# Short filler matmuls, weight and beacon loads asked for in another order, and query copies of batch 1 on ScalarE, in a fused beacon attention and maxout FFN kernel

## The chip, the cores and the metric

The kernel runs on one core of a Trainium2 chip. The metric is device time in microseconds, the median of several runs. The engines are called as the profile calls them: PE (TensorE, matmuls; PEld is its weight loads), ACT (ScalarE), DVE (VectorE), POOL (GpSimd) and SP (SyncE, here an issuer of DMAs). Each works through its own instructions in order, and they meet at semaphores.

## The reference

Attention over 8 batches of 8 heads, 576 tokens of 64 features, with 16 beacon keys and values in front of each head's own, causal over the own ones; then an FFN over 4608 tokens whose hidden layer is the largest of three products.

```python
def _attn_ref(q, k, v, beacon_k, beacon_v):      # B, H, S, Nb, D = 8, 8, 576, 16, 64
    scale = 1.0 / np.sqrt(D)
    k_all = np.concatenate([beacon_k, k], axis=2)
    v_all = np.concatenate([beacon_v, v], axis=2)
    scores = scale * np.matmul(q, k_all.transpose(0, 1, 3, 2))
    causal[:, Nb:] = np.triu(np.ones((S, S), dtype=bool), k=1)
    scores = np.where(causal, -1000000000.0, scores)
    scores = scores - scores.max(-1, keepdims=True)
    a = np.exp(scores)
    a /= a.sum(-1, keepdims=True) + 1e-09
    return np.matmul(a, v_all)

def _moe_ref(x, w1, w2, w3, w_out):              # 4608 tokens, 512 -> 768 -> 512
    h = np.maximum(np.maximum(x @ w1, x @ w2), x @ w3)
    return h @ w_out
```

All inputs and the output are float32; the kernel's matmuls are in bfloat16.

## The kernel before

**Tiling.** Two heads are a pair (four pairs a batch, numbered through: pairs 0 to 3 are batch 0, 4 to 7 batch 1), four heads a quad. For a pair, queries and keys come from HBM with tokens on the partitions and are turned by PE transposes into qT and kT (features on the partitions); the turned tile is in a PSUM bank and is copied to SBUF by DVE or ACT. Scores come out with keys on the partitions (L505 in batch 0, L520 later), ACT takes the exponential of a whole group of banks into `at_sb` (L514, L538), and masks zero what is above the diagonal: POOL with an affine select (L560), or DVE with a product by a triangle (L558, batch 0 only). For a quad, PE forms the sums of the weights, with a block of ones as stationary operand, and the products with the values (L609 in batch 0, L642 later). ACT gets the reciprocal of the sums by Ln and Exp (L675 and L676, or L658 to L660), and DVE multiplies it in and leaves the attention output in `xT` (L686, L665), which is already the layout that the FFN wants. The FFN works on blocks of 512 tokens in units: mm1 units (L710, in halves L739 for the first block) with a running maximum in `hT` by DVE (L728, L751; the first of the three products is only cast, L730, L753), and mm2 units (L762) whose result is copied to `y` and stored.

**Order.** Nothing is scheduled by a program: the order in which the Python code emits instructions is the order on each engine, and it is written out by hand. `start()` loads and turns the first two pairs of batch 0. `first_batch()` is a list of calls: `S_` scores and exponential of a pair's group, `T` (`turn_part`) a half turn of a pair, `M` masks (a third argument True puts them on DVE), `P` (`emit_pv`) sums and value products of a quad's half, `V(t)` (`cast_first_v`) the cast of value tile t by POOL, `F` an FFN unit. `second_batch()` goes over pairs 4 to 7: beacon keys of the next pair copied by ACT, a burst of scores with five exponentials, masks on POOL, the turn of the next pair, two or three FFN units; then sums and products of quad 2 (`emit_pv_whole`) and the turn of pair 8. From pair 8 on a loop does the same with a plan of loads and casts, and there the query copy of a turned pair is by ACT already.

**Queues around the change.** POOL casts the values, masks, and also issues the DMAs that cast on their way from float32 to bfloat16: `load_w(i, [g])` (half g of FFN weight i, L344), `load_cast(p)` (queries and keys of pair p, L258). SP issues the value loads (L301, L306) and the beacon keys of batches 1 to 3 (L353), which POOL casts at L968. What POOL waits for holds up all that stands behind it in its list, asks for DMAs included.

**Fillers.** `fill(at_bank, n)` (L413) runs n matmuls of a tile of ones into a PSUM bank that is about to be overwritten; `turn_part` calls it with `idle` 1 in four places (L920, L923, L928, L935), and `first_batch` with 2 in two (L941, L950).

**Turned queries.** `turn_pair(p, q_copy)` (L458) takes two banks, emits 24 transposes, has DVE copy the keys (`evac_k`, L453) and `q_copy` the queries (`evac_q`, L442). `second_batch` gives it `by_dve`. `emit_pv_whole` (L623) emits the matmuls of a quad, then three ACT copies of the products to `raw` (L652, L653), then Ln, Ln and Exp on ACT (L658 to L660), and returns `finish`, which emits the two multiplies on DVE.

Of the kernel before, what the change touches and what calls it, by code (L numbers as in the profile page):

```python
# [17 lines left out]
def kernel(  # L18
# [41 lines left out]
    n_quad = 2  # L60
    PPB = H // 2
# [41 lines left out]
    def head(g, j):  # L103
        return 4 * g + j

    def place(p):
        b, pi = divmod(p, PPB)
        return b, pi // PPQ, 2 * (pi % PPQ)
# [15 lines left out]
    acc = psum.tile([128, N_BANK, 512], FP32, name="acc")  # L124
# [20 lines left out]
    def next_bank():  # L145
        i = free_banks.pop(0)
        free_banks.append(i)
        return i
# [18 lines left out]
    def next_psum(dtype=FP32):  # L167
        view = acc[:, next_bank()]
        return view if dtype == FP32 else view.bitcast(dtype)
# [9 lines left out]
    bk32_1 = const.tile([NB_PE - Nb, H, D], FP32, name="bk32_1")  # L179
    bk16_1 = const.tile([NB_PE - Nb, H, D], BF16, name="bk16_1")  # L180
# [3 lines left out]
    busy = const.tile([128, 512], BF16, name="busy")  # L184
# [20 lines left out]
    by_dve = nc.vector.tensor_copy  # L205
    by_act = nc.scalar.copy
    by_pool = nc.gpsimd.tensor_copy
# [46 lines left out]
    def load_cast(p):  # L254
        b, g, j0 = place(p)
        for i, src in enumerate((q, k)):
            t16 = quads[g][i][:, 2 * j0 : 2 * j0 + 4]
            nc.gpsimd.dma_start(  # L258
                out=t16.rearrange("p (h s) r d -> p h (s r d)", h=2),
                in_=src[b, head(g, j0) : head(g, j0) + 2].rearrange("h (p r) d -> p h (r d)", r=QR),  # L260
            )
            rows = t16.rearrange("p (h s) r d -> p h (s r) d", h=2)
            stage["pair16", p, i] = (rows[:, 0], rows[:, 1])
# [77 lines left out]
    def load_w(i, gs=range(n_quad)):  # L341
        wv = (moe_w1, moe_w2, moe_w3)[i].rearrange("(g p e) f -> g p e f", g=n_quad, e=2)
        for g in gs:
            nc.gpsimd.dma_start(out=w_in[i][:, 2 * g : 2 * g + 2], in_=wv[g])  # L344
# [66 lines left out]
                )  # L411

    def fill(at_bank, n):  # L413
        for _ in range(n):
            nc.tensor.matmul(
                acc[:, at_bank], busy[:, 0:128], busy, start=True, stop=True
            )

    def turn_part(p, h, i, at_bank, copy=None, idle=0):
# [31 lines left out]
    def evac_k(p, ps, copy):  # L451
        kT = kTs[p % NT]
        copy(  # L453
            kT[:, Nb:NK].rearrange("d (p r) -> d p r", r=QR),
            ps.rearrange("d (r p) -> d p r", r=QR),
        )

    def turn_pair(p, q_copy):  # L458
        banks = [next_psum(BF16)[:, 0:S] for i in range(2)]
        for i in range(2):  # L460
            turn(p, i, banks[i])
        evac_k(p, banks[1], by_dve)
        evac_q(p, banks[0], q_copy)
# [156 lines left out]

    products = []

    def emit_pv_whole(quad):  # L623
        b, g = divmod(quad, n_quad)
        v_sb = v_tiles[b]
        for p in range(PPQ * quad, PPQ * (quad + 1)):
            assert all((p, gi) in masked for gi in range(NG))
        banks = [next_bank() for _ in range(4)]
        runs = [(part, banks[part], 0, HEAD, S) for part in range(3)]
        runs += [(part, banks[3], part * HEAD, 0, HEAD) for part in range(3)]  # L630
        for part, bank, lo, qa, qb in runs:
            ts = [t for t in range(n_kt) if q_min[t] < qb]
            for t in ts:
                q0 = max(qa, q_min[t])
                n = k_rows[t]
                for j in range(4):
                    lhsT = (
                        ones[0:n]
                        if part == 0
                        else v_sb[0:n, t, head(g, j), part - 1 : D : 2]  # L640
                    )
                    nc.tensor.matmul(  # L642
                        acc[32 * j : 32 * j + 32, bank, lo + q0 - qa : lo + qb - qa],
                        lhsT,
                        at_view(PPQ * quad + j // 2, t, j % 2, q0, qb),
                        start=(t == 0),
                        stop=(t == ts[-1]),
                        tile_position=(0, 32 * j),
                    )
        raw = pv_pool.tile([128, 2, S], FP32, name="raw")  # L650
        for part in (1, 2):
            nc.scalar.copy(raw[:, part - 1, HEAD:S], acc[:, banks[part]])  # L652
        nc.scalar.copy(  # L653
            raw[:, :, 0:HEAD],
            acc[:, banks[3], HEAD : 3 * HEAD].rearrange("p (i c) -> p i c", i=2),
        )
        recip = nrm_pool.tile([128, S], FP32, name="recip")
        nc.scalar.activation(out=recip[:, HEAD:S], in_=acc[:, banks[0]], func=AF.Ln)  # L658
        nc.scalar.activation(out=recip[:, 0:HEAD], in_=acc[:, banks[3], 0:HEAD], func=AF.Ln)
        nc.scalar.activation(out=recip, in_=recip, func=AF.Exp, scale=-1.0)  # L660

        def finish():
            c0 = b % RING * S
            for i in range(2):
                nc.vector.tensor_mul(xT[:, 2 * g + i, c0 : c0 + S], raw[:, i], recip)  # L665
            if g == n_quad - 1:
                ready[0] = 2 * b + 1

        return finish
# [168 lines left out]
    def L(fn, *a):  # L838
        return lambda: fn(*a)
# [68 lines left out]
    def first_batch():  # L908
        S_(0, 0)
        T(2, 0, 0, 6)  # L910
        T(3, 0, 0, 4)
        load_v(0, 0, nc.vector)
        load_v(0, 1)
        load_beacons(1, B_PE, bk32_1)
        S_(1, 0)
        T(2, 0, 1, 7)
        T(3, 0, 1, 5)
        M(0, 0, True)
        S_(2, 0)
        T(0, 1, 0, 6, None, 1)  # L920
        T(1, 1, 0, 4)
        S_(3, 0)
        T(0, 1, 1, 7, None, 1)  # L923
        T(1, 1, 1, 5)
        M(1, 0, True)
        S_(0, 1)
        V(0)
        T(2, 1, 0, 6, None, 1)  # L928
        T(3, 1, 0, 4)
        load_w(0, [0])  # L930
        S_(1, 1)
        M(2, 0, True)
        V(1)
        load_w(0, [1])
        T(2, 1, 1, 7, None, 1)  # L935
        T(3, 1, 1, 5)
        M(3, 0, True)
        S_(0, 3)
        V(2)
        S_(0, 2)  # L940
        fill(6, 2)  # L941
        S_(1, 3)
        for p in range(PPB):
            M(p, 1)
        M(0, 3, True)
        M(0, 2, True)
        V(3)
        V(4)
        S_(1, 2)
        fill(6, 2)  # L950
        S_(2, 1)
        M(1, 3, True)
        M(1, 2, True)
        S_(3, 1)
        load_w(1, [0])
        P(0, 0, apart=True)
        S_(2, 3)
        load_w(1, [1])
        M(2, 3)
        S_(2, 2)  # L960
        M(2, 2)
        P(0, 1, 0, 2)
        S_(3, 3)
        M(3, 3, True)
        P(0, 1, 2)
        S_(3, 2)
        M(3, 2, True)
        by_pool(bk16_1, bk32_1)  # L968
        load_cast(PPB)
        load_cast(PPB + 1)  # L970
        load_cast(PPB + 2)
        load_w(2)
        load_cast(PPB + 3)
        P(1, 0, tiles=sc_psum.tile())
        P(1, 1, tiles=sc_psum.tile())
        for quad, hf in ((0, 0), (1, 0), (0, 1), (1, 1)):
            invert_sums(quad, hf)
            multiply()
            if (quad, hf) == (0, 1):
                F()  # L980
        F(2)
        turn_beacons(1, B_PE, bk16_1)
        place_beacons(PPB, by_act)
        F(2)
        free_banks[:] = [4, 5, 0, 1, 2, 3, 7, 6]
        turn_pair(PPB, by_act)
        load_v(1, 0, nc.vector)
        load_v(1, 1)
        F(1, next_psum)

    def second_batch():
        for p in range(PPB, 2 * PPB):
            place_beacons(p + 1, by_act)
            emit_burst(p)
            if p == PPB + 2:
                load_cast(2 * PPB)
                load_w_out()
                load_cast(2 * PPB + 1)
            for gi in range(NG):
                emit_masks(p, gi)  # L1000
                if p == PPB + 2 and gi == 1:
                    cast_v(1, 0, by_pool)
            if p == PPB + 2:
                next_load(gate=nc.gpsimd)
                next_load(4)
                cast_v(1, 1, by_pool)
            if p + 1 < 2 * PPB:
                turn_pair(p + 1, by_dve)
                F(2, next_psum)
                if p < PPB + 2:  # L1010
                    F(1, last_pair(), True)
        F(2, next_psum)
        finish = emit_pv_whole(n_quad)
        turn_pair(2 * PPB, by_dve)
        F(2, next_psum)
        finish()

# [92 lines left out]
```

## Time and profile before

| | us |
|---|---|
| runs, median of 3 | 284.77 (284.46 to 284.79) |
| profiled execution, device time | 286.59 |
| profiled execution, span of the instructions | 284.9 |

The span is the time from the first to the last instruction of the program; the device time of the same execution has 1.7 us around it. The TensorE clock that was granted is 1.00 in every stage. The stages of the profiled execution, as busy microseconds of each engine:

| stage, us from the start | PE | DVE | ACT | POOL |
|---|---|---|---|---|
| 7 to 16: first scores and turns of batch 0 | 7.75 | 8.67 | 8.45 | 2.15 |
| 16 to 22: sums and products of batch 0 | 4.66 | 1.23 | 4.58 | 3.97 |
| 22 to 26: up to the first FFN unit | 2.04 | 3.08 | 2.36 | 2.32 |
| 26 to 45: FFN units, pairs 4 to 6 | 18.57 | 13.25 | 11.38 | 11.58 |
| 45 to 60: pair 7, quads 2 and 3 | 14.75 | 8.32 | 12.68 | 10.93 |
| 60 to 270: the rest of the loop | 210.00 | 128.32 | 117.58 | 98.04 |

How lines of the profile are read: in a timeline, the first number is the start in us and the second how long the group took; then engine, line, operation, the tile written and the tile read by the program's names, the partitions and elements, and how many instructions the group merges (the shape is that of the first). In brackets stands how long the engine had been idle before, and what released it, as far as semaphore events show; where that had long been done, it was something else. In the DMA part, a queue's line gives packets, megabytes and its share of the time of 16 DMA engines. POOL's and SP's DMA lines give the time to issue; the landing comes later.

### The profile page before, as it was taken

What the parts mean: (1) busy time and instruction counts of PE and PEld (TensorE: products, weight loads), DVE (VectorE), ACT (ScalarE), POOL (GpSimd) and SP (SyncE); (2) the same over time, 40 slices, a digit from 0 to 9 for tenths busy, and PEclk for the clock granted to TensorE, in tenths of its full rate; (3) what the DMA queues carried; (4) which work ended last, traced back from release to release, by engine and by line L of the source; (5) the groups of instructions that cost most, each with busy time, mean ns of one, the idle gap of its engine ahead of it and who ended that gap; (6) DMA issues with size and microseconds to landing.
All of it is one profiled execution on the core that took longest, in us unless ns stands there. A gap on an engine that the chain in (4) does not pass through costs nothing.

```text
span 284.9 us, 7772 instructions
## 1 busy us (share of the span) xinstructions
PE 274.5 (96%) x3075; PEld 157.3 (55%) x3075; DVE 173.7 (61%) x311; ACT 159.9 (56%) x299; POOL 134.2 (47%) x277
## 2 busy tenths in 40 slices
PE   7976999999999999999999999999999999999994
PEld 3545774555555555555556787555555554444442
DVE  4936785564765748373837383638364847776872
ACT  3975568895668585858585858575766640000000
POOL 7167359558486775457455836583336210000000
PEclk9999999999999999999999999999999999999999
DMA  8999999999998999979999999979845003003004
GB/s 139 204 165 166 170 211 144 239 175 294 286 209 213 226 257 193 183 185 275 252 223 193 257 210 203 205 183 267 206 104 171 0 2 147 4 0 147 2 0 147
DMA packets 85316, 48.84 MB, mean 171 GB/s; under 512 B 64416, under 2 KB 80032, under 8 KB 85280
## 3 DMA queue, kind: packets, MB, share of 16 engines
q1 hardware_dynamic: 78176, 42.22, 65.5%
q0 software_dynamic: 6544, 5.80, 13.9%
q8 instruction: 24, 0.39, 0.6%
q10 hardware_dynamic: 560, 0.33, 0.5%
q14 instruction: 12, 0.10, 0.2%
HBM read 35.13 MB, written 14.22 MB: 173 GB/s over the span
## 4 chain that ended last, share of the span: by engine, by line
PE 81%; DVE 1%; issue 0%; DVEq 0%
PE acc L710 45%; PE acc L762 16%; PE acc L642 11%; PE acc L520 7%; PE acc L406 2%; PE acc L780 0%; DVE hT L728 0%; DVE y L787 0%; DVE qT L442 0%; DVE kT L453 0%; DVEq L453 0%
## 5 line engine op out<-in xcount | busy, mean ns | idle before, releaser
L710 PE MATMUL acc<-xT,w_sb 128*128 128x512 bf16 (+4 forms) x744 | 135.5, 338 | 0.1
L728 DVE TENSOR_TENSOR hT<-hT,acc 128x512 bf16<-128x512 bf16 x102 | 70.0, 688 | 58.2 <-PE acc L710 53.2
L710 PEld LDWEIGHTS <-w_sb 128*128 128x128 bf16 x744 | 69.2, 98 | 59.6
L560 POOL TENSOR_SCALAR_AFFINE_SELECT at_sb<-at_sb 128x256 bf16<-128x256 bf16 (+1 forms) x171 | 61.9, 384 | 81.0 <-ACT at_sb L538 79.8
L538 ACT ACTIVATE at_sb<-acc 128x208 bf16<-128x208 f32 (+3 forms) x140 | 89.5, 737 | 6.7 <-PE acc L520 5.5
L762 PE MATMUL acc<-w_out_sb,hT 128*128 128x512 bf16 (+2 forms) x246 | 48.4, 348 | 0.0
L277 POOL CAST p<-st 96x768 bf16<-96x768 f32 x44 | 34.9, 822 | 0.0
L769 DVE COPY y<-acc 128x512 f32<-128x512 f32 (+1 forms) x35 | 22.0, 629 | 21.2 <-PE acc L762 14.9
L762 PEld LDWEIGHTS <-hT 128*128 128x128 bf16 x246 | 22.6, 98 | 21.7 <-DVE hT L728 1.6
L730 ACT CAST hT<-acc 128x352 bf16<-128x352 f32 x18 | 8.1, 452 | 47.0 <-PE acc L710 47.0
L730 DVE CAST hT<-acc 128x512 bf16<-128x512 f32 (+1 forms) x48 | 26.6, 554 | 9.9 <-PE acc L710 9.6
L520 PE MATMUL acc<-qT,kT 64*128 64x208 bf16 (+1 forms) x336 | 26.6, 280 | 0.4 <-DVE hT L728 0.2
L787 ACT COPY y<-acc 128x320 f32<-128x320 f32 x1 | 0.4, 425 | 46.0 <-PE acc L780 46.0
L642 PE MATMUL acc<-at_sb,v_sb 128*32 128x512 bf16 (+5 forms) x672 | 22.8, 281 | 0.0
L520 PEld LDWEIGHTS <-kT 64*128 64x128 bf16 x336 | 15.4, 94 | 12.7 <-issue 2.5
L665 DVE TENSOR_TENSOR xT<-raw,recip 128x576 bf16<-128x576 f32 x28 | 21.1, 796 | 0.0
L642 PEld LDWEIGHTS <-v_sb 128*32 128x32 bf16 (+1 forms) x672 | 14.6, 97 | 6.7
L322 POOL CAST v_sb<-st 128x1536 bf16<-128x1536 f32 (+2 forms) x21 | 18.3, 894 | 0.0
L652 ACT COPY raw<-acc 128x512 f32<-128x512 f32 x28 | 15.8, 637 | 2.6 <-PE acc L642 2.4
L642 PE MATMUL acc<-at_sb,ones 128*32 128x512 bf16 (+3 forms) x336 | 14.9, 284 | 0.0
L514 ACT ACTIVATE at_sb<-acc 128x1024 bf16<-128x1024 f32 (+2 forms) x16 | 13.1, 864 | 2.6 <-PE acc L505 2.5
L453 DVE COPY kT<-acc 128x576 bf16<-128x576 bf16 x12 | 9.0, 754 | 5.7 <-PE acc L406 4.5
(73 smaller groups left out, 179.4 us busy)
## 6 DMA issues: line engine op xcount, KB each, us to landing
out_dram<-y SPq DMA_DIRECT2D x35, 256.0 KB, 3.5
st<-in_q_dram SPq DMA_DIRECT2D x22, 288.0 KB, 4.4
st<-in_k_dram SPq DMA_DIRECT2D x22, 288.0 KB, 4.7
st<-in_v_dram SPq DMA_DIRECT2D x24, 256.0 KB, 6.0
w_sb<-in_moe_w_dram POOLq DMA_DIRECT2D x6, 384.0 KB, 7.8
q_dram<-p SPq DMA_DIRECT2D x16, 144.0 KB, 2.6
k_dram<-p SPq DMA_DIRECT2D x16, 144.0 KB, 2.5
st<-in_v_dram SPq DMA_DIRECT2D x8, 224.0 KB, 6.2
```

The source lines that it names most:

```text
L277: cast(t16.rearrange("p r h d -> p h r d"), st[0:QP, i * NQ2 : (i + 1) * NQ2].rearrange("p (h r d) -> p h r d", h=2, r=QR),)
L322: cast(v_sb[0:n, t:t1].rearrange("p t h d -> p (t h d)"), st[0:n, (t - t_lo) * H * D : (t1 - t_lo) * H * D],)
L520: nc.tensor.matmul(ps, kTs[p % NT][hs, 128 * t : 128 * t + 128], qTs[p % NT][hs, q0:q1], start=True, stop=True, tile_position=(64 * e, 0),)
L538: nc.scalar.activation(out=both_heads(p, gi)[:, e0:e1], in_=acc[:, first + e0 : first + e1, 0 : g_width(p, gi)], func=AF.Exp, scale=scale,)
L560: nc.gpsimd.affine_select(out=view, in_=view, compare_op=ALU.is_ge, fill=0.0, base=x0, pattern=[[0, 2], [1, hi - lo]], channel_multiplier=-1,)
L642: nc.tensor.matmul(acc[32 * j : 32 * j + 32, bank, lo + q0 - qa : lo + qb - qa], lhsT, at_view(PPQ * quad + j // 2, t, j % 2, q0, qb), sta ...
L665: nc.vector.tensor_mul(xT[:, 2 * g + i, c0 : c0 + S], raw[:, i], recip)
L710: nc.tensor.matmul(ps[:, a:b], w_in[i][:, ct, 128 * ft : 128 * (ft + 1)], xT[:, ct, x0 : x0 + b - a], start=(ct == 0), stop=(ct == n_ct - 1),)
L728: nc.vector.tensor_max(h[:, lo:hi], h[:, lo:hi], ps[:, lo:hi])
L730: (by_act if hi < TOKB else by_dve)(h[:, lo:hi], ps[:, lo:hi])
L762: nc.tensor.matmul(ps[:, lo:hi], hT[:, ft, 128 * tt : 128 * (tt + 1)], w_out_sb[:, ft, lo:hi], start=(ft == 0), stop=(ft == n_ft - 1),)
L769: (by_act if hi < d_model else by_dve)(y[:, lo:hi], ps[:, lo:hi])
```

## The change

It has four parts. (1) A filler of 512 columns becomes four of 128, each into its own quarter of the bank; all have a weight load of their own. (2) In `first_batch` the first half of weight 1 (`load_w(0, [0])`) is asked for behind `V(1)` and no longer ahead of the second scores of pair 1; so it moves behind that cast on POOL. (3) The halves of weight 2 (`load_w(1, ...)`) move by a few calls to either side of the masks `M(2, 3)` and `M(2, 2)`, and the beacon cast moves behind the casting loads of pairs 4 and 5. (4) In `second_batch` the turned queries of pairs 5 to 8 are copied by ACT; the turn of pair 8 is now emitted from inside `emit_pv_whole`, so that on ACT its copy stands between the copies to `raw` and the logarithms.

```diff
     def fill(at_bank, n):
-        for _ in range(n):
+        for i in range(4 * n):
+            x0 = 128 * (i % 4)
             nc.tensor.matmul(
-                acc[:, at_bank], busy[:, 0:128], busy, start=True, stop=True
+                acc[:, at_bank, x0 : x0 + 128],
+                busy[:, 0:128],
+                busy[:, 0:128],
+                start=True,
+                stop=True,
             )
...
-    def emit_pv_whole(quad):
+    def emit_pv_whole(quad, after_raw=None):
...
             acc[:, banks[3], HEAD : 3 * HEAD].rearrange("p (i c) -> p i c", i=2),
         )
+        if after_raw:
+            after_raw()
         recip = nrm_pool.tile([128, S], FP32, name="recip")
...
         T(3, 1, 0, 4)
-        load_w(0, [0])
         S_(1, 1)
         M(2, 0, True)
         V(1)
+        load_w(0, [0])
         load_w(0, [1])
...
         S_(3, 1)
-        load_w(1, [0])
         P(0, 0, apart=True)
         S_(2, 3)
-        load_w(1, [1])
+        load_w(1, [0])
         M(2, 3)
         S_(2, 2)
         M(2, 2)
+        load_w(1, [1])
         P(0, 1, 0, 2)
...
-        by_pool(bk16_1, bk32_1)
         load_cast(PPB)
         load_cast(PPB + 1)
+        by_pool(bk16_1, bk32_1)
         load_cast(PPB + 2)
...
             if p + 1 < 2 * PPB:
-                turn_pair(p + 1, by_dve)
+                turn_pair(p + 1, by_act)
                 F(2, next_psum)
                 if p < PPB + 2:
                     F(1, last_pair(), True)
         F(2, next_psum)
-        finish = emit_pv_whole(n_quad)
-        turn_pair(2 * PPB, by_dve)
+        finish = emit_pv_whole(n_quad, L(turn_pair, 2 * PPB, by_act))
         F(2, next_psum)
         finish()
```

## The prediction

> **What bounds it now.** I read first the page's busy shares, its slices and its DMA queues, then the timelines of PE, ACT, POOL and DVE up to 60 us, then the DMA view in narrow windows.
>
> ```profile
> span 284.9 us, 7772 instructions
> PE 274.5 (96%) x3075; PEld 157.3 (55%) x3075; DVE 173.7 (61%) x311; ACT 159.9 (56%) x299; POOL 134.2 (47%) x277
> PE   7976999999999999999999999999999999999994
> q8 instruction: 24, 0.39, 0.6%
> ```
>
> From the fourth slice on PE is the bound: whatever brings PE to its first FFN matmul (L739, 26.27 us) earlier comes off the end, unless a later wait eats it. Up to 26 us PE waits for others, and there most of the edits lie. The POOL timeline of that stretch:
>
> ```profile
> 13.77 0.56 POOL L344 DMA_DIRECT2D w_sb<-in_moe_w_dram  x1
> 15.00 0.61 POOL L334 CAST v_sb<-st 128x512 bf16<-128x512 f32 x1 [0.68 <-DMA st<-in_v_dram]
> 15.55 0.55 POOL L344 DMA_DIRECT2D w_sb<-in_moe_w_dram  x1
> 16.09 1.36 POOL L334 CAST v_sb<-st 128x512 bf16<-128x512 f32 x2
> 19.48 0.61 POOL L334 CAST v_sb<-st 80x512 bf16<-80x512 f32 x1 [2.03 <-DMA st<-in_v_dram]
> 20.03 1.06 POOL L344 DMA_DIRECT2D w_sb<-in_moe_w_dram  x2
> 23.74 0.60 POOL L968 CAST bk<-bk 48x512 bf16<-48x512 f32 x1 [1.68 <-DMA bk<-in_beacon_k_dram]
> ```
>
> The fifth value cast waits 2.03 us for its DMA. PE, ACT and DVE in the same stretch:
>
> ```profile
> 20.14 0.22 PE L609 MATMUL acc<-at_sb,v_sb 80*32 80x80 bf16 x4 [0.49 <-POOL v_sb L334]
> 20.72 1.30 ACT L514 ACTIVATE at_sb<-acc 128x992 bf16<-128x992 f32 x2 [1.24 <-PE acc L505]
> 21.75 0.76 DVE L558 TENSOR_TENSOR at_sb<-at_sb,tri 128x160 bf16<-128x160 bf16 x3 [4.77 <-ACT at_sb L514]
> 22.44 0.63 PE L609 MATMUL acc<-at_sb,ones 128*32 128x288 bf16 x14
> 25.03 0.27 PE L609 MATMUL acc<-at_sb,ones 128*32 128x208 bf16 x4 [1.96 <-DVE xT L686]
> 26.27 2.86 PE L739 MATMUL acc<-xT,w_sb 128*128 128x256 bf16 x24
> ```
>
> The largest wait, 1.96 us, is in the middle of the row sums of P(1, 1). DVE is named, but these matmuls read no xT, and the masks that they do read were done at 21.75 + 0.76 = 22.51. So I look for something else, and find it in queue q8. Its 24 packets of 0.39 MB are 16 KB each; PE has 3075 matmuls and 3075 weight loads, and 6150 / 24 = 256 to a packet. Counted along the timeline, the wait sits behind matmul 352 and its load, some 706 instructions in, and the narrow DMA windows show q8 packets at 11.92, 22.78 (until 23.73), 26.80 and 35.62 us. I read the wait as PE's **instruction block** coming late: it ends 1.30 us after the second packet does. Blocks of 256 then end at 194, 450 and 706, if 62 instructions run ahead of the program's first (706 + 62 = 3 x 256), which no row shows. PE came past 450 at 18.77, at the earliest 18.3 by its waits, and the packet started 4.5 us later; for the next five it is 4.5, 5.0, 1.4, 4.2 and 4.5.
>
> In batch 1:
>
> ```profile
> 42.30 3.20 ACT L538 ACTIVATE at_sb<-acc 128x208 bf16<-128x208 f32 x5 [1.26 <-PE acc L520]
> 44.45 0.75 DVE L442 COPY qT<-acc 128x576 bf16<-128x576 bf16 x1
> 45.34 0.24 ACT L449 COPY kT<-bT 128x16 bf16<-128x16 bf16 x1
> 45.58 1.23 PE L520 MATMUL acc<-qT,kT 64*128 64x208 bf16 x12
> 54.30 0.36 PE L520 MATMUL acc<-qT,kT 64*128 64x336 bf16 x5 [0.20 <-DVE hT L728]
> ```
>
> The query copy of pair 7 is done at 45.20, before its scores at 45.58; ACT is busy with exponentials until 45.50.
>
> **The change, part by part.**
>
> *Fillers.* Eight of 512 columns (L415 x8) become 32 of 128. Two in a row take 0.60 us where one takes 0.387: 213 ns each, start to start. For 128 columns with a weight load each there is no row. L406 with 96 columns gives (680 - 206) / 11 = 43 ns, L739 with 256 gives (2860 - 273) / 23 = 112 ns. Between them I take 57: four are 228, so 15 ns more a filler, 0.12 us in all; bounds 8 x (172 - 213) = -0.33 and 8 x (448 - 213) = +1.9 us. PE waits for exponentials right behind them, 0.21, 0.39 and 0.53 us at 14.45, 15.92 and 18.34, and ACT is busy 8.45 of 9.00 us from 7 to 16: on the path 0 at 57 ns, and 1.9 - 1.1 = 0.8 at the upper bound. But they add 24 matmuls and 24 loads, 48 PE instructions, ahead of everything from 15 us on.
>
> *Weight 1 behind V(1).* POOL would now do V(1) at 15.00, both asks at 15.55 and 16.10, V(2) and V(3) from 16.65 to 18.0. These two casts are 0.56 later, and P(0, 0) wants the third value tile at about 16.85: PE stops there until 17.33. The cover is ACT, whose exponentials run on to 19.48; the scores behind it come at 17.9, before their exponential is due at 18.2: 0, or 0.5 without that cover. On the DMA side, value packets fall from 601 in the microsecond at 14 to 156 and 16 in the next two, as soon as the first weight packets come (49 and 60 of 3 KB). Some 730 value and 384 beacon packets are then left; at 800 a microsecond, the rate at 10 to 14, they are through at 16.5, ahead of the weight's first packets at 15.55 + 1.2. So V(4) follows V(3), 18.0 to 18.6 in place of 19.48 to 20.09. The 0.49 wait at 20.14 goes, and exponentials, sums and P(1, 0) come 0.5 earlier. Weight 1 lands at 16.8 + 0.79 MB / 0.19 to 0.20 MB per us = 20.7 to 21.0 (23.25 before), well before L739.
>
> *Weight 2, casting loads, beacon cast.* POOL: half of weight 2 at 18.6, masks at 19.2, the other half at 20.1, four casting loads of 0.64 each from 20.65, the beacon cast at 23.2 (23.74 before), which PE wants at 29.07. Nothing is later. The transposes at 31.33 show no wait for their loads, so nothing is won either.
>
> *The instruction block.* With 48 more instructions the block ends fall on what were 402 and 658. 402 lies in P(0, 0) behind the third value tile: PE passes it at 17.33, 1.0 earlier than 18.3. 658 lies at the end of P(1, 0), reached at some 22.2 - 0.5 = 21.7. The packet asked for at 17.33 stands behind all of weight 1, which drains at 20.7 to 21.0; I take 21.0 (bounds: 1.4 behind the request, 18.7, and 5.0 behind it, 22.3). PE goes on 0.95 + 1.30 later, at 23.25. From there it has 0.25 of P(1, 0) and 1.85 of P(1, 1) to do: L739 at 25.35, 0.92 before 26.27. The reciprocal of (1, 0), which now starts after the stop, needs 0.25 + 0.1 + 0.41 + 0.44 + about 1 of multiplies = 2.2 and is wanted 2.4 after it by the last of the first unit's four matmuls: it just fits.
>
> *Copies by ACT.* Pairs 5 and 6: exponentials end at 36.4 and 40.9, the copy (0.62 to 0.69) and the beacon copy at 37.2 and 41.8, the scores start at 37.46 and 41.94: no cost. Pair 7 has two FFN units between, not three: the copy runs 45.36 to 46.0, scores at 46.06 in place of 45.58, +0.48; the bank wait inside them (0.14) goes, and DVE, 0.75 freer, takes 0.08 out of the scores of pair 5. Pair 8: ACT does the copy at 51.6 before the logarithms, which end at 53.56, just before the exponentials at 53.65; DVE's two hT steps start 0.5 earlier, so the wait at 54.30 goes, -0.29 (from 54.30 back to the matmul before it are 0.50 us, and 0.21 where such a pair doesn't wait). Net 0.48 - 0.14 - 0.08 - 0.29 = -0.03, between -0.5 and +0.5.
>
> **Sum:** -0.92 - 0.03 = -0.95 us: span 284.9 to 283.95, the profiled execution's 286.59 to 285.64. The median of the runs, 284.77, is 1.8 below that; I take the same difference off it: **283.8**.
>
> [...]
>
> **Rivals.**
>
> 1. *The stop follows what the profile names.* For it: the first xT multiply of (0, 1) starts at 24.67, and may end just before 25.03. Against it: that product is not read there. The stop would then come with the reciprocals, 0.5 earlier through V(4): 284.77 - 0.5 = 284.3.
> 2. *Slower: the block is as late as before, and stops more.* Weight 1's halves now stand in the queues as one run, right before the request. If the packet starts at 22.78 again, PE goes on at 25.03 from 658, not 706, with 2.1 to do in place of 1.24: +0.86, 285.6. It decides from a packet at 21.9 on. For it: 4.5 to 5.0 in most of the loaded cases. Against: values and beacons, which shared the engines from 17 to 23, are through by then.
> 3. *No stop:* the packet starts by 19.4. L739 follows P(1, 1) at 23.07 + 1.25 - 0.5 = 23.8, -2.4: 282.4. For it the 1.4 case; against it a queue full of weights.
>
> **Chances.** Forecast 0.43, first rival 0.2, second 0.2, third 0.17. 0.2% is 0.57 us, about what a measurement of this kernel can tell from no change. Faster by more: the third, most of the forecast, a little of the first: 0.58. Within: 0.23. Slower: 0.19, the second. The forecast's own range is 283.2 to 284.5 (packet at 20.4 to 21.7); the range is 282.4 to 285.5, which takes in rivals 1 and 3 and the 0.8 of the fillers' bound, and leaves out the worst of the second.
>
> **What would show it.** Right: the fifth value cast at about 18 us with no DMA wait; the q8 packet at about 21; a PE stop inside P(1, 0), not in P(1, 1), ending near 23.3; L739 near 25.3; the scores of pair 7 waiting some 0.5 for an ACT copy; no wait in those of pair 8. Wrong: the stop still at the same matmul, a cast of V(4) that still waits, or a later stop of PE that gives the gain back.

## The result, and the profile after

The kernel became slower: 287.43 us, the median of 15 runs (285.55 to 289.63), against 285.13 of 15 runs of the kernel before (284.46 to 286.28). The ratio of the means is 1.0065, with a 95% interval of 1.0037 to 1.0092. The forecast was 283.8, and the time lies above its range.

And yet the profiled execution of the changed kernel looks much as forecast: span 284.3 us against 284.9, device time 286.00 against 286.59. Its page:

```profile
span 284.3 us, 7821 instructions
PE 274.2 (96%) x3099; PEld 158.1 (56%) x3099; DVE 171.7 (60%) x307; ACT 162.1 (57%) x303; POOL 134.5 (47%) x277
PE   7987999999999999999999999999999999999994
q8 instruction: 24, 0.39, 0.6%
```

PE has its 24 matmuls and 24 loads more, ACT four copies more, DVE four fewer; the share of PE and the slices have hardly moved. POOL's timeline:

```profile
15.43 1.11 POOL L344 DMA_DIRECT2D w_sb<-in_moe_w_dram  x2
16.52 1.89 POOL L334 CAST v_sb<-st 128x512 bf16<-128x512 f32 x3
18.35 0.53 POOL L344 DMA_DIRECT2D w_sb<-in_moe_w_dram  x1
23.25 0.62 POOL L977 CAST bk<-bk 48x512 bf16<-48x512 f32 x1
```

The last three value casts are one run of 1.89 us with no DMA wait in it; before, the fifth stood 2.03 us. PE's timeline:

```profile
21.36 0.53 PE L614 MATMUL acc<-at_sb,v_sb 128*32 128x288 bf16 x18
23.44 0.33 PE L614 MATMUL acc<-at_sb,v_sb 128*32 128x176 bf16 x8 [1.56 <-issue]
25.23 2.86 PE L746 MATMUL acc<-xT,w_sb 128*128 128x256 bf16 x24
30.37 0.39 PE L746 MATMUL acc<-xT,w_sb 128*128 128x256 bf16 x2 [0.23 <-issue]
45.44 0.89 PE L525 MATMUL acc<-qT,kT 64*128 64x208 bf16 x12 [0.42 <-ACT qT L447]
52.80 1.21 PE L525 MATMUL acc<-qT,kT 64*128 64x208 bf16 x12
```

The stop has moved from P(1, 1) into P(1, 0) and is 1.56 us, with nothing to be seen that PE waits for ("issue"); the q8 packets start at 11.55, 21.08, 28.02 and 34.05 us. The first FFN matmul is at 25.23 (26.27 before). A second, small stop has come at 30.37. The scores of pair 7 wait 0.42 for ACT's copy, and the wait at 54.30 is gone.

So the two profiled executions say 0.6 us faster and the medians 2.3 slower. What lies between is in the list of all runs. The difference of device time and span is about 1.75 us in all of them. The kernel before has spans around 283.4 us, and its profiled execution (span 284.9, device time 286.59) lies above all 15 of its runs. The changed kernel has 7 runs around 284.3 at a granted clock of 1.00, and 8 at 285.7 to 287.9 whose mean clock is 0.994 or less.

### The profile page after: what moved, and what is told of

The parts are those of the page before. It is cut to its first block, busy times and chain, and to the rows that moved or that the text cites. A ratio compares the mean times of both kernels' runs of the same rounds, so it can differ in the third digit from the quotient of the medians.

```text
span 284.3 us, 7821 instructions
## 1 busy us (share of the span) xinstructions
PE 274.2 (96%) x3099; PEld 158.1 (56%) x3099; DVE 171.7 (60%) x307; ACT 162.1 (57%) x303; POOL 134.5 (47%) x277
## 4 chain that ended last, share of the span: by engine, by line
PE 90%; ACT 5%; DVE 2%; DMA 1%; issue 1%
PE acc L717 46%; PE acc L769 16%; PE acc L647 11%; PE acc L525 8%; PE acc L746 3%; ACT at_sb L519 3%; PE acc L406 2%; DMA bk<-in_beacon_k_dram 1%; PE acc L614 1%; ACT at_sb L543 1%; DVE hT L760 1%; PE acc L510 1%; PE acc L787 0%; DVE qT L440 0%; DVE xT L693 0%
## 5 line engine op out<-in xcount | busy, mean ns | idle before, releaser
L322 POOL CAST v_sb<-st 128x1536 bf16<-128x1536 f32 (+2 forms) x21 | 18.3, 898 | 0.0
```

## The experiments

Line numbers shift by up to nine between the kernels. The runs are of three chips (r1 to r4, r5 to r15, r16 and r17); the kernel before was timed beside them on each, with a median span of 283.2 to 283.6 at full clock. The span of the runs at full clock (median) and the number of runs that lost the clock (mean granted clock of 0.994 or less) are worked out from the list of every run's span and clock.

**r1 and r2: both kernels once more**, for a second profile and second times of each. No edit.

> The kernel before, unchanged, to see the spans and clocks of its single runs. Theory A (the profiled execution of before was not a usual one: its stop of 1.96 us for an instruction block is shorter in the usual run): most spans near 283.4, which is the median 285.13 less the 1.7 us that lie around a span, and under the 284.9 of the profile; clock 1.000 in most. Theory B (the clock): before has clock 1.000 in 12 or more of 15 runs, so that the loss of the changed kernel is in its runs at 0.994. Rival C (waits for ACT in batch 1 are the loss): spans and clocks of before tell nothing of it.

> The changed kernel again. Theory B: about half of the runs at clock 0.994, about 2 us longer than those at 1.000 (286.3 against 284.4 in span). Theory A: the runs at 1.000 stay at spans of 284.3, near that of the profile. Ratio to before about 1.0065 again.

Measured: r1 285.39 us, ratio 0.9999 [0.9985, 1.0012], none of 12 runs lost the clock, spans 283.2 to 284.2. r2 286.08, ratio 1.0046 [1.0021, 1.0071], 3 of 12 lost it; at full clock 284.20. PE in r1:

```profile
20.83 0.22 PE L610 MATMUL acc<-at_sb,v_sb 80*32 80x80 bf16 x4 [0.58 <-POOL v_sb L335]
22.46 0.41 PE L610 MATMUL acc<-at_sb,ones 128*32 128x288 bf16 x12 [0.30 <-ACT at_sb L515]
23.13 0.75 PE L610 MATMUL acc<-at_sb,ones 128*32 128x288 bf16 x20
24.82 2.35 PE L740 MATMUL acc<-xT,w_sb 128*128 128x256 bf16 x17
```

In this execution of the unchanged kernel **there is no stop**. The row sums of P(1, 1) run through from 23.13, where the other profile stood 1.96 us, and the first FFN matmul is at 24.82. Its packet started at 20.65, not at 22.78. The wait for the fifth value cast is there (0.58). Span 283.7, near the median of before: this execution is a usual one by its span, and the profile that I predicted from was not. r2 repeats the changed kernel's picture: packet 21.24, stop 1.49 ending at 23.70, first FFN matmul 25.49.

**r3: long fillers in the changed kernel; r4: short fillers alone in the kernel before.**

```diff
 r3                                   r4
-        for i in range(4 * n):      -        for _ in range(n):
+        for _ in range(n):          +        for i in range(4 * n):
```

> The changed kernel with the fillers of before (8 of 512 columns), all else changed. Theory B, with the short fillers as the cause of the lower clock: clock 1.000 in nearly all runs, and no run above 287. Theory A says nothing of the clock, but the block end goes back to its place in P(1, 1), and with its request later: L739 0 to 0.7 us later than in the changed kernel where the stop shows. Rival C: still slower than before by 0.3 to 0.5 at clock 1.000.

> The kernel before with the short fillers alone. Theory B: a lower clock in about half of the runs, 2 us longer there; median 286 to 287.5. If short fillers are not the cause: clock 1.000 as in before, and a change by the block end's place alone, within 1 us either way.

Measured: r3 285.78, ratio 1.0019 [1.0001, 1.0036], 284.10 at full clock, 1 of 12 lost it; the stop is back at the old place in P(1, 1), 1.04 us, ending at 23.60 (packet 21.22). r4 285.64, ratio 1.0016 [0.9995, 1.0037], 283.65 at full clock, 4 of 12 lost it. So the rest of the change without short fillers has most of the loss at full clock (284.10 against 283.4) and little trouble with the clock; short fillers without the rest cost 0.25 there, within what this can tell, but lose the clock. Neither run went as theory B had it: r3 has a run above 287, and r4's median is under 286. r3's profile, with a span of 283.5, is among the fastest of its runs at full clock (283.5 to 284.6), so it does not show where the usual 284.10 goes. r4's profile is of an execution that lost the clock:

```profile
21.99 0.22 PE L614 MATMUL acc<-at_sb,v_sb 80*32 80x80 bf16 x4 [1.70 <-POOL v_sb L334]
```

In the table by windows (window, its length, busy us of PE, PEld, DVE, ACT and POOL, granted clock, DMA share, GB/s):

```profile
20.00:22.00 2.00, 0.30 (x16) 0.03 (x8) 0.00 (x0) 0.12 (x1) 0.68 (x2) 1.00 0.73 140
22.00:23.00 1.00, 1.00 (x20) 0.55 (x24) 0.00 (x0) 0.23 (x1) 1.00 (x3) 0.58 0.04 6
23.00:25.00 2.00, 2.00 (x72) 1.61 (x64) 1.01 (x3) 1.65 (x4) 2.00 (x5) 0.50 0.95 144
25.00:26.00 1.00, 1.00 (x44) 0.87 (x36) 0.69 (x3) 0.97 (x3) 1.00 (x3) 0.71 1.13 218
```

PE stands 1.70 us up to 21.99 for the fifth value cast. Then the clock is at a half: 0.58 in the microsecond at 22 means from 22.16, 0.71 at 25 means up to 25.58. That is 3.42 us at half speed right behind a stop, and this stop is no instruction block's.

**r5: 24 two-column matmuls more in the fillers of the kernel before; r6: the same on top of the changed kernel.** r5 moves the block ends by 48 instructions as the change does, with hardly any work; r6 moves them by 96.

```diff
-            nc.tensor.matmul(acc[:, at_bank], busy[:, 0:128], busy, ...)
+            for cols in (512, 2, 2, 2):
+                nc.tensor.matmul(acc[:, at_bank, 0:cols], busy[:, 0:128], busy[:, 0:cols], ...)
```

> The kernel before with its 8 long fillers, and behind each three matmuls of 2 columns: 48 PE instructions more, as the short fillers bring, but the fillers' 512 columns stay. Theory D (the place of the block end is the loss: with 48 more instructions it lies in P(1, 0), PE stops there until the block is in at about 23.5, and has 1.8 to 2.1 us of work left before the first FFN matmul, not 1.2): as with short fillers alone, a median 285.4 to 286.2, first FFN matmul 25.0 to 25.6 in the profile, and a clock of 0.994 or less in 2 to 6 of 12 runs, because PE is idle there. Rival E (short matmuls themselves count as less work and let the clock fall): no run under 0.996, median within 0.3 of before.

> The changed kernel with 24 more matmuls of 2 columns among its short fillers, 48 further PE instructions: the block end moves on to the start of P(1, 0). Theory D: PE stops there until about 23.4 and has some 0.45 us more to do after it than in the changed kernel; first FFN matmul near 25.7, spans at clock 1.000 0.3 to 0.6 longer than the 284.3 of the changed kernel. Rival C (batch 1's waits for ACT are the loss): as the changed kernel.

Measured: r5 285.25, ratio 1.0003 [0.9988, 1.0019], 283.50 at full clock, 1 of 13 lost it. r6 288.32, ratio 1.0115 [1.0091, 1.0139], 4 of 6 lost it, 286.0 at full clock. So 48 instructions more cost next to nothing in the order of before, and theory D, which had 285.4 to 286.2 for r5, missed; in the changed kernel another 48 cost 1.7 at full clock, where it had 0.3 to 0.6. r5's profile is of the one execution that lost the clock: PE waits 1.37 us for the fifth value cast, up to 21.79, comes to the block end only at 24.27, when the packet of 21.86 is long in, and does not stop there. PE in r6:

```profile
22.87 0.25 PE L615 MATMUL acc<-at_sb,ones 128*32 128x176 bf16 x4 [0.57 <-issue]
29.24 0.83 PE L747 MATMUL acc<-xT,w_sb 128*128 128x256 bf16 x6 [2.01 <-issue]
```

The packets start at 20.59 and 26.62. The first stop has become short, because its packet came early; the second is now 2.01 us, in the middle of an FFN unit and again with no engine named. (The 286.0 is of two runs only.)

**r7: the changed kernel without fillers; r8: with the query copies by DVE again.**

```diff
 r7                       r8
     def fill(at_bank, n):  -                turn_pair(p + 1, by_act)
+        return             +                turn_pair(p + 1, by_dve)
                            -        finish = emit_pv_whole(n_quad, L(turn_pair, 2 * PPB, by_act))
                            +        finish = emit_pv_whole(n_quad)
                            +        turn_pair(2 * PPB, by_dve)
```

> The changed kernel without fillers (they compute nothing that is used): 64 PE instructions fewer than in it, 16 fewer than before; the block end lies 16 instructions further on in P(1, 1) than before. Theory D: a stop of at most 1 us that leaves about 1.0 of work; first FFN matmul 24.5 to 24.8; spans at 1.000 of 283.0 to 283.8. Rival E: without any filler PE is idle longer from 9 to 16 us, and the clock falls in more runs than in the changed kernel (11 of 27), in windows before 20 us.

> The changed kernel with the copies of batch 1's turned queries back on DVE. Theory D and my sum (-0.03 us for these copies): the same as the changed kernel within 0.3 us at clock 1.000, the wait of 0.42 for ACT at 45.44 gone and the waits at the bank in its scores and in those of pair 8 back. Rival C: 0.4 us or more faster at clock 1.000, near 283.8.

Measured: r7 285.66, ratio 1.0019 [1.0007, 1.0031]; all 12 runs lose the clock (0.988 to 0.994), with a median span of 283.95. In its profile (span 283.1, mean clock 0.993) the matmuls are slow before 20 us, as rival E had it: 20 row sums at 18.46 take 1.15 us, where r13 takes 0.68 for the same 20 at 18.84. At full clock PE has a wait of 0.53 for exponentials there (r13, 18.67), which r7 doesn't have, and the stop at the block end is 0.20. So the fillers do hold the clock: with them 3 of 12 runs of the changed kernel lost it in r2, without them 12 of 12. Where it fell in the other 11 runs is not seen, but by the spans the loss costs little there. r8 286.07, ratio 1.0051 [1.0026, 1.0077], 284.15 at full clock, 4 of 12 lost it. That is the changed kernel within 0.15 us, as theory D had it: the copies are worth about nothing either way.

**r9 and r10: half of weight 1 later.** If the packet is late because it is queued behind weight 1, less of weight 1 ahead of it should bring it sooner. r9 is the changed kernel, r10 is r3 (long fillers), both with

```diff
         V(1)
         load_w(0, [0])
-        load_w(0, [1])
...
         V(3)
+        load_w(0, [1])
         V(4)
```

> The changed kernel with the second half of weight 1 asked for between V(3) and V(4), not between S_(2,2) and S_(2,3). Theory (the packet of instructions comes at about 21 because it is queued behind the DMAs of weight 1's two halves, and TensorE goes on 2.3 us after it comes): with half as much weight asked ahead of it the packet comes at 18.5 to 20.3, the stop at the block end shrinks from 1.5 to under 0.7 us, the first FFN matmul is at 24.0 to 24.6, the span at full clock falls from 284.2 to 283.2 to 283.7, and at most 2 of 12 executions lose the clock. Rival (the packet is late for something other than weight 1): packet still at 21.0 to 21.3, stop 1.4 us or more, span at full clock 284.0 to 284.4.

> As r9, with the fillers as eight long matmuls (r3 with the later half). Theory: 24 instructions fewer lie ahead of the block end, so TensorE gets there later, and with the packet at 18.5 to 20.3 there is no stop there; first FFN matmul at 23.6 to 24.3 against 24.84 in r3; span at full clock 282.8 to 283.5 against 284.1 in r3, and no or one execution loses the clock: the time 284.6 to 285.2, level with before or 0.1% below it. Rival: packet at 21.2 as in r3, stop of 1 us, span at full clock 284.0.

Measured: r9 285.03, ratio 0.9979 [0.9961, 0.9997]; 283.15 at full clock against 284.2 to 284.3 of the changed kernel, 2 of 14 lost it. r10 286.04, ratio 1.0036 [1.0015, 1.0056], 284.30, 2 of 12. Both profiles fell on executions that lost the clock, and both have a late packet: 21.99 with a stop of 1.82, and 22.32 with 2.15. So r9's span came out as expected and the packet in its profile did not; r10 missed both.

**r11 and r12: two more profiles of the changed kernel**, unedited, to see where the clock falls.

> The changed kernel as it is, one profile, to see where the clock falls in those of its executions that lose it. [...] If the clock does not fall, span 284.0 to 284.5.

> [...]

Measured: r11 span 283.9 at full clock, packet 21.18, stop 1.52. r12 span 288.5 (286 to 287 was expected), clock 0.986, packet 23.40 and a stop of 3.00 us. r12 by PE's timeline and by windows:

```profile
22.06 0.53 PE L615 MATMUL acc<-at_sb,v_sb 128*32 128x288 bf16 x18
25.59 0.48 PE L615 MATMUL acc<-at_sb,v_sb 128*32 128x176 bf16 x8 [3.00 <-issue]
```

```profile
21.00:24.00 3.00, 1.28 (x66) 0.98 (x55) 1.48 (x6) 2.76 (x7) 3.00 (x6) 1.00 1.09 214
24.00:25.00 1.00, 0.00 (x0) 0.00 (x0) 0.00 (x0) 0.67 (x2) 1.00 (x3) 0.78 1.09 191
28.00:30.00 2.00, 2.00 (x43) 1.56 (x33) 0.00 (x0) 0.85 (x2) 0.67 (x2) 0.50 1.30 204
31.00:32.00 1.00, 1.00 (x10) 0.82 (x8) 1.00 (x3) 0.00 (x0) 0.91 (x2) 0.81 1.19 218
```

From 22.59 to 25.59 PE does nothing. The clock falls at 24.56 (0.78 in that microsecond) and comes back at 31.38 (0.81): 6.82 us, twice the length seen in r4. The first FFN matmul is at 28.91, so 1.0 us of it lies on the stop, 3.3 on the sums and products of P(1, 0) and P(1, 1), which PE runs without a wait, and 2.5 on the first FFN unit. Here the stop comes first and the clock goes while PE still stands: **the clock can go in or right behind a stop of PE**, here the packet's, in r4 the one for the fifth value cast. In r5 the matmuls are slow from 23.64 on (26 in 1.11 us, 0.77 in r13), 1.85 us behind the end of that stop. In r9, r10 and r14 the half clock begins within the packet's stop: by the tables by windows at 24.00 in r9, with the stop from 22.46 to 24.28, at 24.66 in r10 (22.57 to 24.72) and at 24.60 in r14 (23.07 to 24.67), and it lasts 3.42 us in r9 and r10 and 3.4 in r14.

How busy PE was does not tell the stops with a fall from those without. In the 3.42 us just ahead of the fall PE was busy 33% of the time in r12, 38% in r10, 43% in r4, 46% in r9 and 47% in r14. But the profile predicted from held the clock with 38% (21.61 to 25.03), and the profile after with 46% (20.02 to 23.44). What decides is not shown.

**r13, r14, r15: r9 timed again, and one more profile each of r10 and r9.**

> The kernel of r9 once more. If its gain is real: ratio to before 0.9965 to 0.9995, span at full clock 282.9 to 283.4 against 283.2 to 283.5 of before, at most 3 executions lose the clock. If r9 was luck: ratio 1.000 to 1.004, span at full clock 283.6 to 284.2. In a profile at full clock the theory (packet, then 2.3 us) has TensorE go on 2.2 to 2.6 us after its packet, wherever that comes, with a stop under 1 us and the first FFN matmul at 24.0 to 24.8.

> The kernel of r10, one profile. Span 283.9 to 284.4 at full clock, 286 to 286.6 if it loses the clock. Theory: TensorE goes on 2.2 to 2.6 us after the third packet if it stands at the block end; what r10 has lost to r9 (1.1 us of span) is then seen as a longer stop there, or at the next block end near 30. Rival: no stop longer than r9's, and the loss lies in another stage, in waits that are not of the block.

> The kernel of r9, one profile. [...]

Measured: r13 284.73, ratio 0.9992 [0.9975, 1.0009]; none of 12 lost the clock, 283.05 against 283.30 of before. r14 span 286.1, clock lost, packet 22.40, stop 1.60 ending at 24.67. r15 284.2 at full clock. r13 and r15 are one and the same kernel, both profiles at full clock, and they show what the stop hangs on. PE in r13, then in r15:

```profile
21.42 0.41 PE L616 MATMUL acc<-at_sb,ones 128*32 128x288 bf16 x12 [0.30 <-ACT at_sb L521]
21.64 0.77 PE L616 MATMUL acc<-at_sb,v_sb 128*32 128x288 bf16 x26
23.87 3.02 PE L748 MATMUL acc<-xT,w_sb 128*128 128x256 bf16 x24
```

```profile
21.43 0.41 PE L616 MATMUL acc<-at_sb,ones 128*32 128x288 bf16 x12 [0.30 <-ACT at_sb L521]
21.65 0.53 PE L616 MATMUL acc<-at_sb,v_sb 128*32 128x288 bf16 x18
23.73 0.33 PE L616 MATMUL acc<-at_sb,v_sb 128*32 128x176 bf16 x8 [1.55 <-issue]
25.52 2.76 PE L748 MATMUL acc<-xT,w_sb 128*128 128x256 bf16 x23
```

Up to 21.42 and 21.43 they are the same to 0.01 us. r13's packet started at 19.78: the 26 matmuls run through, and nothing stops. r15's started at 21.41: after 18 of them, at instruction 706, PE stands 1.55 us and goes on 2.32 after the packet's start. The spans are 282.7 and 284.2, apart by just that stop. (The expected "under 1 us" thus held in one of the two.) r14, the order with long fillers, has a stop of 1.60 where r13 has none.

**r16 and r17: weight 1's first half asked for where the kernel before does it, the second behind V(3)**, timed, with a second profile as r17.

```diff
         T(3, 1, 0, 4)
+        load_w(0, [0])
         S_(1, 1)
         M(2, 0, True)
         V(1)
-        load_w(0, [0])
-        load_w(0, [1])
...
         V(3)
+        load_w(0, [1])
         V(4)
```

> The changed kernel with the first half of weight 1 asked for where the kernel before does it and the second half between V(3) and V(4). If weight 1's DMAs set the packet's time: packet at 18.5 to 20.5, so TensorE may go on by 20.8 to 22.9 and finds no stop or one under 0.7 us; no execution, or one, loses the clock; span at full clock 282.7 to 283.3, ratio to before 0.996 to 1.000. If the packet's time is scatter: packet anywhere from 20.5 to 22, stop of 1 us and more in the profile, spans from 282.7 to 284.4 with executions that lose the clock. If the first half so early delays the fifth value tile again, V(4) waits for its DMA as in the kernel before (0.49 in PE at 20), which gives 0.3 to 0.5 back.

> The kernel of r16, one more profile, with the same expectations; in it as in every run with a stop at that block end TensorE goes on 2.2 to 2.6 us after the packet starts.

Measured: r16 285.29, ratio 1.0003 [0.9988, 1.0017], 283.55 at full clock against 283.60 of before; none of 12 lost the clock. The packets start at 19.19 (r16) and 18.31 (r17), the earliest seen, and neither profile has a stop at the block end. But in r16:

```profile
20.90 0.22 PE L615 MATMUL acc<-at_sb,v_sb 80*32 80x80 bf16 x4 [0.92 <-POOL v_sb L335]
24.81 3.18 PE L747 MATMUL acc<-xT,w_sb 128*128 128x256 bf16 x24
```

The fifth value cast is waited for again, 0.92, as in the kernel before. r17 didn't have that wait: first FFN matmul 24.04, span 283.0. In r16 moving weight 1 has traded one wait for the other, and in the median this split gains nothing on the kernel before.

## Why the prediction was wrong, point by point

**What the executions at full clock show together.** "Back" is when PE goes on behind the stop, "left" the span less the start of the first FFN matmul.

| profile | packet | back | stop | first FFN matmul | span | left |
|---|---|---|---|---|---|---|
| before, as predicted from | 22.78 | 25.03 | 1.96 | 26.27 | 284.9 | 258.6 |
| r1, before | 20.65 | | none | 24.82 | 283.7 | 258.9 |
| after | 21.08 | 23.44 | 1.56 | 25.23 | 284.3 | 259.1 |
| r2, after | 21.24 | 23.70 | 1.49 | 25.49 | 284.3 | 258.8 |
| r11, after | 21.18 | 23.41 | 1.52 | 25.20 | 283.9 | 258.7 |
| r8, copies by DVE | 21.29 | 23.69 | 1.61 | 25.47 | 284.1 | 258.6 |
| r3, long fillers | 21.22 | 23.60 | 1.04 | 24.84 | 283.5 | 258.7 |
| r15, later half | 21.41 | 23.73 | 1.55 | 25.52 | 284.2 | 258.7 |
| r13, later half | 19.78 | | none | 23.87 | 282.7 | 258.8 |
| r17, halves split | 18.31 | | none | 24.04 | 283.0 | 259.0 |
| r16, halves split | 19.19 | | none | 24.81 | 284.4 | 259.6 |
| r6, 96 more | 20.59 | 22.87 | 0.57 | 25.03 | 285.7 | 260.7 |

But for r6 with its second stop of 2.01 and r16 (a wait of 0.29 for a load of keys at 31.00; the rest of its 0.8 is not traced to a wait), what comes behind the first FFN matmul takes 258.6 to 259.1 in all of them: in these profiles the kernels differ by when that matmul starts.

*The stop is an instruction block:* right. In every profile with a stop there, full clock or not, PE is back 2.2 to 2.5 us after that packet starts, for packets from 20.59 to 23.40. In the profile after, PE passes 22 of its 24 block ends without a stop that is put down to "issue", and stops at two, for 1.56 and 0.23 us. In the prediction's own profile the packet, 22.78 to 23.73, comes while PE stands (23.07 to 25.03) and ends 1.30 us ahead of the stop's end.

*Where the block ends move, packet at 21.0, on again at 23.25, first FFN matmul at 25.35:* right in number; 21.08, 23.44 and 25.23. But the 21.0 came by luck: it was the time at which all of weight 1 would be in, and in the profile after its halves landed at 20.4 and 23.4, the second 2.3 us behind the packet. The distances from a block end to a packet, which gave the bounds, were also counted from the earliest moment that PE's waits allowed; from the instruction at the block end itself they are 4.0 us, and 1.8, 3.8, -0.3, 3.3 and 3.0 for the next five. That PE asks for a packet as it passes a block end was my estimate from these distances; no run shows it.

*V(4) without its wait, fillers at no cost, weight 2 and beacons at no cost:* right in the profile; eight short fillers in a row take 0.62 us and one 0.219, so 57 ns each, as taken.

*Copies by ACT, -0.03:* right in size as far as can be told, since r8 and r2 have 284.15 and 284.20; the +0.48 at pair 7 (0.42) and the gain at pair 8 are there as forecast.

*The sum, span 283.95:* measured 284.3, and 284.2 to 284.3 in the median at full clock. The 0.35 is in part the next block end, the stop of 0.23 at 30.37, which I didn't look for. I forecast one block's time and stopped counting.

**The step that failed** is the last one of the sum: "The median of the runs, 284.77, is 1.8 below that; I take the same difference off it". Those 1.8 us were mostly the stop itself. The profiled execution had it, and the usual ones, going by their spans, don't: r1 without it has a span of 283.7, and of 128 executions of before at full clock one reaches 284.9, with a median of 283.4. So the stop was taken off twice, once as the gain of the change, and once in the difference to the median. The changed kernel has its stop in the usual execution too, as all four of its profiles show. Without that subtraction the forecast would have been 285.64, against 286.0 measured at full clock. The rivals' prices are set against the same 284.77. In the usual execution the change removes the wait for V(4), some 0.5, and PE comes to the block end that much sooner and with 48 instructions fewer to go, 21.9 in place of 23.5. But it cannot pass before 23.4, since the packet still comes at 21.1, and from there it has 1.8 us to the FFN, not 1.3. I had this as the second rival, with "from a packet at 21.9 on" as its point. Against a usual execution it decides far earlier: r1 comes past the block end at 23.52, and 706 is followed there by 1.30, so in the changed kernel any packet from some 20.7 on is a loss (24.82 - 1.79 - 2.36).

**What wasn't in it at all** is the clock. A stop of PE can cost more than its own length: in r9, behind one of 1.82 us, another 1.48. In 12 of 29 executions of the changed kernel whose clock was listed, the mean clock is 0.994 or less, which is what 3.42 us at half come to, or more (1.7 of 286 is 0.6%). The kernel before lost it in 4 of 132. Where the half clock lies is seen in one of the 12, r12: from within the stop on (24.56 to 31.38), for the most part on work that PE runs without a wait. From the stop's end to the first FFN matmul r9's profile takes 3.27 us, where r15, the same kernel at full clock, takes 1.79. An execution at 0.994 is some 2.0 us longer (286.3 against 284.3), and how much of that is the clock and how much a later packet was not separated. At 8 of 15 runs the median itself is such a run, and this is the difference of 286.0 and 287.43.

**What stays open.** The same kernel has its packet at 21.08 to 23.40 (four profiles), r9's at 19.78 to 21.99 (three). That it waits in a queue behind weight 1 fits much of this and was not shown. In r13 and r15 weight 1's first half is asked for at 15.51 and 15.52 and lands 4.9 and 6.3 us later, and the packet starts 0.6 and 0.4 us ahead of that landing; in r16 and r17, with the half asked for earlier, 0.2 and 0.3 ahead; but in the four profiles of the changed kernel 0.5 to 1.0 behind it, and in r3 0.7 ahead. In r10 and r14, with long fillers, PE passes the block end before (instruction 450) at 18.9 and 19.5, 1.3 to 1.4 us after the second half was asked for, and in r13 and r15 0.3 us ahead of it; a request that stands behind the second half would explain packets at 22.3 and 22.4, but no run tests it. Nor is it shown where r3's usual 284.10 goes. r9's order beat the changed kernel by about 1.0 us of span both times; that it beats the kernel before is not settled (0.9979 [0.9961, 0.9997], then 0.9992 [0.9975, 1.0009]).

## What to carry to other kernels

One profiled execution may be an unusual one: before a stall in it is counted as a gain, its span should be held against the list of spans of the plain runs, and a difference between the two is not to be subtracted a second time. Work that makes PE arrive earlier at a point that something else releases gains nothing there, and loses what it moved behind that point; here the release was an instruction packet, and 48 instructions' shift and a wait of 0.5 us less moved PE's arrival by 1.6. And a stop of PE can have a second price, the clock after it, which r9 paid (1.82 us of stop, then 3.27 in place of 1.79 up to the FFN) on work that PE runs without a wait, as r12 did (3.00, then 3.32).

## What the runs showed of the hardware that was not expected

- The second of PE's instruction packets in the span came at 18.3 to 23.4 us and took 0.9 to 1.4 us, and where PE stood at the block end, it went on 2.2 to 2.5 us after the packet's start (2.6 at the next block end in r6). No run shows that the packet waits its turn with the data.
- The profile gives such a stop to "issue", or to some engine that happened to end just then (DVE xT in the profile predicted from and in r3, r10 and r14). The count of PE instructions, a multiple of 256 less 62 at every one of these stops, is the surer sign.
- The granted clock fell to a half for 3.42 us in r4, r9 and r10, 3.4 in r14 and 6.82 in r12, in or right behind stops of 1.70, 1.82, 2.15, 1.60 and 3.00 us; in r5, with a stop of 1.37, the slow matmuls begin 1.85 us behind it. But 1.96 in the profile predicted from, 2.01 in r6 and 1.49 to 1.61 in five others had no such fall. The length of the stop does not decide alone, and what else does is not shown.
- Without any filler the clock fell in 12 of 12 runs, and yet the median span, 283.95, was below that of the changed kernel with the clock held.
